# First tile of a fused retention and two-expert-layer kernel: unread products of zeros, k's decays by TensorE, small transfers on ScalarE's queue, v and the next k loaded ahead of the decay matrix

## The chip, the cores and the metric

One program on one core of a Trainium2 chip (8 cores). The metric is the device time of one execution in microseconds (us); the time before is a median of three executions. The profile is one further execution, taken with the hardware profiler.

The engines are TensorE (PE in the rows; PEld is its weight load), VectorE (DVE), ScalarE (ACT), GpSimd (POOL) and SyncE (SP). "SPq" marks an instruction in which SyncE issues a transfer (DMA). Each engine runs its own instructions in the order in which they are written; an instruction waits until its operands are ready, and all behind it on that engine wait too.

## The reference

Inputs: q, k, v of shape (2, 8, 768, 64), one decay `lam` per head, and the weights of two mixture layers of 8 experts. All is float32.

```python
for b in range(nb):                       # blocks of one sequence (block = 64)
    intra = einsum(qb, kb) * Dmask        # Dmask[i, j] = lam ** (i - j) for i >= j, else 0
    intra = einsum(intra, vb)
    inter = einsum(qb * lam ** (pos + 1), kv_state)
    out[block] = intra + inter
    kb_dec   = kb * lam ** (block - 1 - pos)
    kv_state = lam ** block * kv_state + einsum(kb_dec, vb)
x = out as (1536, 512)
...
logits = x @ w_gate + softplus(x @ w_noise) * noise    # first layer: the best two experts of each row
x = sum over the two of weight * relu(x @ w1[e]) @ w2[e]
...
x = gate * relu(x @ u1[e]) @ u2[e]                     # second layer: the best one, with a capacity
```

## The kernel before, in words

The sequence stage treats 12 tiles of 128 rows (6 for each of the two sequences), with blocks of 128 instead of 64, which computes the same. For tile j the steps are, by the names that the rows show:

- loads of k, q and v (`ldk`, `ldq`, `ldv`; one `ldq` serves two tiles), issued by SyncE, with three buffers for k and v;
- `front(j)`: TensorE transposes k (into the PSUM tile `hp`) and, every second tile, q (`hp<-iw,qp`); ScalarE copies the results to `kT` and `qT`, after bringing q in order (`qp`). GpSimd makes `kd`, which is k times the decays of its rows, and `qd`, which is `qT` times powers;
- `scores(j)`: the products `tr<-qT,kT`; VectorE multiplies them by the decay matrix, `at<-tr,dm`;
- `mix(j)`: the products `yp<-at,ldv` (and, but for the first tile of a sequence, `yp<-qd,st`), which ScalarE copies to `xT`; then `yp<-ldv,kd`, which VectorE adds to the state `st`;
- `rows(j)`: the products `yp<-iw,xT`, which turn the rows back and give the first gate's logits; `xr` is stored to HBM as `x`. `iw` holds the identity and the gates' weights.

`load(j)`, `rows(j - 1)`, `front(j + 1)` and the fetch and conversion of experts' weights (`wst`, loaded by SyncE; ScalarE casts it to `wh`, VectorE makes the rest `wl`) lie between `scores(j)` and `mix(j)`. The order on each engine is made by a scheduler when the kernel is built.

The decay matrix `dm` (128 rows x 8 heads x 128, 512 KB) is built once. `lam` is loaded (`lamb`), VectorE makes its powers by doubling in `pw` (a slice of a buffer called `xg`), SyncE writes 8 rows of them to HBM (`powers`, each followed by a row of zeros), and then reads them back with a start that moves by one element from partition to partition, which gives the matrix with its zeros. The column `dm[:, :, 0:1]` is also what `kd` is made with. `tc.issue_after(x)` sets what follows behind x in the order of issue; it is no wait.

After tile 11 the two expert layers follow, some 560 us of products on TensorE.

Of the kernel before, what the change touches and what calls it, by code (L numbers as in the profile page):

```python
# [20 lines left out]
P = 128  # L21
# [15 lines left out]
def kernel(ctx: ExitStack, tc: tile.TileContext, q, k, v, lam, g1, gn, noise,  # L37
# [105 lines left out]
    def load_v(j):  # L143
        rows_of("v", v, j)

    def load(j):
        load_kq(j)
        load_v(j)
# [14 lines left out]
    nc.gpsimd.affine_select(out=ident, in_=ident, compare_op=OP.not_equal, fill=1.0, base=0,  # L163
                            pattern=[[-1, P]], channel_multiplier=1)
    nc.gpsimd.tensor_copy(iw[:, 1:, G:G + P], ident[:, None, :].to_broadcast([P, DC - 1, P]))


    pw = rt.tile([P, 2, ROW], F32, name="xg", bufs=4).rearrange("p a b -> p (a b)")[:, :H * P]
    pw = pw.rearrange("p (h m) -> p h m", h=H)
    nc.sync.dma_start(powers[:, :, P:], zero[0:1, None, :].to_broadcast([1, H, P]))  # L170
    nc.gpsimd.memset(pw[:, :, P - 1:], 1.0)
    nc.vector.tensor_copy(pw[:, :, P - 2:P - 1], lamb[:, :, None])
    m = 1
    while m < P:
# [2 lines left out]
        nc.vector.tensor_mul(pw[:, :, a - n:a], pw[:, :, P - 1 - n:P - 1],  # L177
                             pw[:, :, a:a + 1].to_broadcast([P, H, n]))
        m *= 2
    written = nc.sync.dma_start(powers[:, :, :P], pw[0:1]).ins  # L180
    with tc.issue_after(written):
        load_v(0)
    dm = aw.tile([P, H, P], F32, name="dm", bufs=1)
    written = nc.sync.dma_start(dm, bass.AP(tensor=powers.tensor, offset=powers.offset,
                                            ap=[[1, P], [2 * P, H], [1, P]])).ins
    with tc.issue_after(written):
        load(1)
    pq = aw.tile([P, HP, P], F32, name="pq", bufs=1)
    dec = consts.tile([P, HP, 1], F32, name="dec")
    half = P // 2  # L190
# [298 lines left out]
    def pair(t, hp):  # L489
        return t[:, 2 * hp:2 * hp + 2, :].rearrange("p a d -> p (a d)")  # L490

    def front_q(j):
# [4 lines left out]
        for g in range(2):  # L497
# [8 lines left out]
            for c in range(2):  # L506
                if j % NC or c:
                    nc.gpsimd.tensor_mul(QD[j][:, hs, c, :], QT[j][:, hs, c, :], pq[:, hs])

    def front_k(j):  # L510
        c = j % NC
        ps = bank("hp", [P, HP, P])
        for hp in range(HP):
            nc.tensor.transpose(ps[:, hp, :], pair(qkv["k", j], hp), ident)
        KT[j] = aw.tile([P, HP, P], F32, name="kT")
        nc.scalar.copy(KT[j], ps)
        if c < NC - 1:
            KD[j] = aw.tile([P, H, D], F32, name="kd")
            kept[j] = nc.gpsimd.tensor_mul(KD[j], qkv["k", j], dm[:, :, 0:1].to_broadcast([P, H, D])).ins

    def front(j):
        front_k(j)
        if j % 2 == 0:
            front_q(j)

    def scores(j):
        qt = QT[j - j % 2]
        ps = [bank("tr", [P, HP, P]) for s in range(2)]
        for hp in range(HP):
            for s in range(2):  # L530
                r = slice(s * D, s * D + D)
                nc.tensor.matmul(ps[s][:, hp, :], KT[j][r, hp, :], qt[r, hp, j % 2, :], start=True, stop=True)
        for s in range(2):
            AT[j, s] = aw.tile([P, HP, P], F32, name="at", bufs=3)
            mixed[j] = nc.vector.tensor_mul(AT[j, s], ps[s], dm[:, s::2, ::-1]).ins
# [123 lines left out]

    tA, tB = slice(0, TA), slice(TA, NT)  # L660
    want(("a", 0), w1[0], w2[0])
    front(0)
    for j in range(NT):
        if j + 2 < NT:
            with tc.issue_after(written):
                load(j + 2)
                if j == 0:
                    nc.sync.dma_start(iw[:, :, :E], g1.rearrange("(c p) e -> p c e", p=P))
                    nc.sync.dma_start(iw[:, :, E:G], gn.rearrange("(c p) e -> p c e", p=P))
                    nc.sync.dma_start(iw[:, :, G + P:], g2.rearrange("(c p) e -> p c e", p=P))  # L670
                    nc.sync.dma_start(nz, noise.rearrange("(t p) e -> p t e", p=P))
        if j == 2:
            with tc.issue_after(kept[1]):
                more_constants()
        scores(j)
        if j:
            rows(j - 1)
        if j + 1 < NT:
# [716 lines left out]
```

## Time and profile before

| | |
|---|---|
| median of 3 executions | 649.7 us (649.18 to 652.34) |
| the profiled execution | 655.0 us, of which 653.2 us are the span from its first to its last instruction |
| TensorE busy | 615.0 us, 94% of the span |
| VectorE / ScalarE / GpSimd busy | 376.1 / 278.9 / 173.9 us |
| granted clock of TensorE, mean of the execution | 0.99 |

Times in the rows are us from the first instruction. A row of the timeline has the start, the busy time, the engine, the line of the kernel, the operation and its tiles (result <- operands), how many instructions are merged into it, and in brackets how long the engine stood idle before it and what ended that. A float32 product of full width shows as two records (x16 for 8 products); a transpose as one.

### The profile page before, as it was taken

To read this page: it belongs to the slowest core of one execution; us is meant where nothing else is said; L and a number is where in the kernel's file an instruction comes from. 1 tells how busy PE (TensorE), PEld (TensorE's weight loads), DVE (VectorE), ACT (ScalarE), POOL (GpSimd) and SP (SyncE) were. 2 spreads that over 40 slices of the span, in tenths; PEclk is the share of its full clock that TensorE was granted. 3 is DMA by queue.
4 is the path that set the end of the run, shared out by engine and by line. 5 is a ranking of instruction groups with operands and counts; after the bars stand their busy time and mean duration, and the time that the engine had idled before them with its cause. 6 is when DMAs were issued, how large, how long until landed. Compare 5 with 4: busy or idle time off the path is not lost. (4 is left out here: it accounts for less than half of the span.)

```text
span 653.2 us, 11244 instructions
## 1 busy us (share of the span) xinstructions
PE 615.0 (94%) x4173; PEld 562.8 (86%) x4173; DVE 376.1 (58%) x841; ACT 278.9 (43%) x481; POOL 173.9 (27%) x197
## 2 busy tenths in 40 slices
PE   3999889989999999999999999999989999999992
PEld 3898877978999999989999999888779989988881
DVE  3375858835545454364544545438777558568880
ACT  2466521135434353343533434135036367466760
POOL 3645610245004021040220101023146135024120
PEclk9999999989999999999999999999999999999997
DMA  6799423355736347565553421182397977757710
GB/s 150 169 300 271 135 85 99 113 160 175 240 98 201 120 113 232 154 185 180 161 168 121 148 66 39 20 294 78 96 335 243 299 239 253 249 192 251 247 38 18
DMA packets 106786, 109.96 MB, mean 168 GB/s; under 512 B 36711, under 2 KB 82807, under 8 KB 106720
## 3 DMA queue, kind: packets, MB, share of 16 engines
q1 hardware_dynamic: 97920, 83.58, 43.0%
q0 software_dynamic: 8800, 25.54, 11.7%
q8 instruction: 36, 0.59, 0.4%
q14 instruction: 30, 0.25, 0.1%
HBM read 92.07 MB, written 17.94 MB: 168 GB/s over the span
## 5 line engine op out<-in xcount | busy, mean ns | idle before, releaser
L111 DVE TENSOR_TENSOR wl<-wst,wh 128x1024 fp32r<-128x1024 f32 x107 | 135.8, 1278 | 60.1 <-ACT wh L105 59.0
L105 ACT CAST wh<-wst 128x1024 fp32r<-128x1024 f32 x107 | 111.4, 1047 | 34.4 <-PE yp L720 28.5
L719 PE MATMUL hp<-x,wh 128*128 128x372 f32 (+9 forms) x352 | 116.9, 333 | 0.8 <-ACTq L1206 0.4
L720 PE MATMUL hp<-x,wh 128*128 128x372 f32 (+9 forms) x352 | 117.2, 334 | 0.0
L721 PE MATMUL hp<-x,wl 128*128 128x372 f32 (+9 forms) x352 | 116.3, 331 | 0.0
L793 ACT ACTIVATE h<-hp 128x372 fp32r<-128x372 f32 (+9 forms) x88 | 41.3, 469 | 172.5 <-PE hp L721 161.3
L719 PE MATMUL yp<-h,wh 128*128 128x372 f32 (+8 forms) x320 | 107.4, 337 | 0.0
L720 PE MATMUL yp<-h,wh 128*128 128x372 f32 (+8 forms) x320 | 106.3, 332 | 1.0 <-DVE h L794 1.0
L721 PE MATMUL yp<-h,wl 128*128 128x372 f32 (+8 forms) x320 | 106.9, 334 | 0.0
L794 DVE SCALAR_TENSOR_TENSOR h<-hp,h 128x372 fp32r<-128x372 f32 (+9 forms) x88 | 46.3, 527 | 64.2 <-ACT h L793 63.5
L719 PEld LDWEIGHTS hp<-x,wh 128*128 128x128 f32 x352 | 66.2, 188 | 2.8 <-issue 0.9
L720 PEld LDWEIGHTS hp<-x,wh 128*128 128x128 f32 x352 | 66.3, 188 | 1.3 <-issue 0.2
L721 PEld LDWEIGHTS hp<-x,wl 128*128 128x128 f32 x352 | 66.2, 188 | 1.3 <-issue 0.9
L469 POOL DMA_INDIRECT xg<-x,Rsrc x25 | 25.6, 1025 | 144.5 <-PE tr L709 125.9
L720 PEld LDWEIGHTS yp<-h,wh 128*128 128x128 f32 x320 | 60.3, 188 | 2.0 <-DVE h L794 1.6
L721 PEld LDWEIGHTS yp<-h,wl 128*128 128x128 f32 x320 | 60.2, 188 | 0.5 <-issue 0.2
L719 PEld LDWEIGHTS yp<-h,wh 128*128 128x128 f32 x320 | 60.0, 188 | 0.7 <-issue 0.4
L711 DVE TENSOR_TENSOR x<-tr,x 128x128 fp32r<-128x128 f32 (+11 forms) x72 | 30.0, 442 | 36.1 <-ACT x L710 31.0
L901 POOL DMA_INDIRECT x<-y,Rdst x25 | 26.2, 1048 | 81.5 <-DVE y L875 77.3
L710 ACT CAST x<-tr 128x128 fp32r<-128x128 f32 (+11 forms) x72 | 26.5, 391 | 44.3 <-PE tr L709 39.4
L866 PE MATMUL tr<-iw,yT 128*128 128x136 f32 (+6 forms) x224 | 35.1, 291 | 2.0 <-DVE y L870 2.0
L866 PEld LDWEIGHTS tr<-iw,yT 128*128 128x128 f32 (+6 forms) x224 | 28.3, 175 | 7.0 <-DVE y L870 2.2
(364 smaller groups left out, 1035.2 us busy)
## 6 DMA issues: line engine op xcount, KB each, us to landing
wst<-in_moe_w_dram SPq DMA_DIRECT2D x107, 512.0 KB
more<-in_moe_w_dram SPq DMA_DIRECT2D x21, 512.0 KB
ldk<-in_k_dram SPq DMA_DIRECT2D x12, 256.0 KB
ldq<-in_q_dram SPq DMA_DIRECT2D x6, 512.0 KB
ldv<-in_v_dram SPq DMA_DIRECT2D x12, 256.0 KB
x<-xr SPq DMA_DIRECT2D x12, 256.0 KB
out_dram<-zero SPq DMA_DIRECT2D x12, 256.0 KB
dm<-powers SPq DMA_DIRECT2D x1, 512.0 KB
```

Of the source, the lines that this page charges most:

```text
L105: nc.scalar.copy(hi, st)
L111: nc.vector.tensor_sub(lo, st, hi.bitcast(F32))
L469: i = nc.gpsimd.indirect_dma_start(out=r, out_offset=None, in_=x, in_offset=bass.IndirectOffsetOnAxis(ap=src(s), axis=0))
L710: a = nc.scalar.copy(hi[:, d, :n], ps[:, :n])
L711: v_ = nc.vector.tensor_sub(lo[:, d, :n], ps[:, :n], hi[:, d, :n].bitcast(F32))
L719: nc.tensor.matmul(ps, a[0], b[0], start=start, stop=False)
L720: nc.tensor.matmul(ps, a[0], b[1], start=False, stop=False)
L721: tail["pe"] = nc.tensor.matmul(ps, a[1], b[0], start=False, stop=stop).ins
L793: tail["act"] = nc.scalar.activation(hh, ps, AF.Relu).ins
L794: tail["dve"] = nc.vector.scalar_tensor_tensor(hl, ps, 0.0, hh.bitcast(F32), op0=OP.max, op1=OP.subtract).ins
L866: nc.tensor.matmul(ps[:m, i, :], self.yT[:, 2 * b + i, s * r:s * r + m], iw[:, 2 * b + i, gates2], start=True, stop=True)
L901: i = nc.gpsimd.indirect_dma_start(out=target, out_offset=bass.IndirectOffsetOnAxis(ap=dst, axis=0), in_=y, in_offset=None, bounds_check=t ...
```

## The change

- Nine products of zeros (`busy(9)`) stand first on TensorE, and six (`busy(6)`) behind the scores of tile 0. Their PSUM bank is read by nobody.
- The decays with which `kd` is made come from 8 products of `pw` with one column of the identity (`decays`), copied by VectorE to `dk`; they stand behind the transposes of the first k. `kd` no longer reads `dm`.
- Four transfers go from SyncE's queue to ScalarE's: the two first gates' weights (16 KB each), the zeros and the powers (4 KB each).
- SyncE issues v of tile 0 and k of tile 1 ahead of `dm`, and `dm` in two halves (one for each parity of the heads) instead of one.

```diff
--- before.py
+++ after.py
@@ -163,11 +163,15 @@
     nc.gpsimd.affine_select(out=ident, in_=ident, compare_op=OP.not_equal, fill=1.0, base=0,
                             pattern=[[-1, P]], channel_multiplier=1)
     nc.gpsimd.tensor_copy(iw[:, 1:, G:G + P], ident[:, None, :].to_broadcast([P, DC - 1, P]))
+    nc.scalar.dma_start(iw[:, :, :E], g1.rearrange("(c p) e -> p c e", p=P))
+    nc.scalar.dma_start(iw[:, :, E:G], gn.rearrange("(c p) e -> p c e", p=P))
 
 
     pw = rt.tile([P, 2, ROW], F32, name="xg", bufs=4).rearrange("p a b -> p (a b)")[:, :H * P]
     pw = pw.rearrange("p (h m) -> p h m", h=H)
-    nc.sync.dma_start(powers[:, :, P:], zero[0:1, None, :].to_broadcast([1, H, P]))
+    nc.scalar.dma_start(powers[:, :, P:], zero[0:1, None, :].to_broadcast([1, H, P]))
+    load_v(0)
+    rows_of("k", k, 1)
     nc.gpsimd.memset(pw[:, :, P - 1:], 1.0)
     nc.vector.tensor_copy(pw[:, :, P - 2:P - 1], lamb[:, :, None])
     m = 1
@@ -177,14 +181,14 @@
         nc.vector.tensor_mul(pw[:, :, a - n:a], pw[:, :, P - 1 - n:P - 1],
                              pw[:, :, a:a + 1].to_broadcast([P, H, n]))
         m *= 2
-    written = nc.sync.dma_start(powers[:, :, :P], pw[0:1]).ins
+    nc.scalar.dma_start(powers[:, :, :P], pw[0:1])
+
+    dm = aw.tile([P, H, P], F32, name="dm", bufs=1)
+    for s in range(2):
+        written = nc.sync.dma_start(dm[:, s::2, :], bass.AP(tensor=powers.tensor, offset=powers.offset + s * 2 * P,
+                                                            ap=[[1, P], [4 * P, HP], [1, P]])).ins
     with tc.issue_after(written):
-        load_v(0)
-    dm = aw.tile([P, H, P], F32, name="dm", bufs=1)
-    written = nc.sync.dma_start(dm, bass.AP(tensor=powers.tensor, offset=powers.offset,
-                                            ap=[[1, P], [2 * P, H], [1, P]])).ins
-    with tc.issue_after(written):
-        load(1)
+        load_v(1)
     pq = aw.tile([P, HP, P], F32, name="pq", bufs=1)
     dec = consts.tile([P, HP, 1], F32, name="dec")
     half = P // 2
@@ -507,16 +511,33 @@
                 if j % NC or c:
                     nc.gpsimd.tensor_mul(QD[j][:, hs, c, :], QT[j][:, hs, c, :], pq[:, hs])
 
+    dk = aw.tile([P, H, 1], F32, name="dk", bufs=1)
+
+    def busy(n):
+
+        ps = bank("yp3", [P, P])
+        for _ in range(n):
+            nc.tensor.matmul(ps, zero, zero, start=True, stop=True)
+
+    def decays():
+        ps = bank("yp2", [P, H, 1])
+        for h in range(H):
+            nc.tensor.matmul(ps[:, h, :], pw[:, h, :], ident[:, 0:1], start=True, stop=True)
+        nc.vector.tensor_copy(dk, ps)
+
     def front_k(j):
         c = j % NC
         ps = bank("hp", [P, HP, P])
         for hp in range(HP):
-            nc.tensor.transpose(ps[:, hp, :], pair(qkv["k", j], hp), ident)
+            i = nc.tensor.transpose(ps[:, hp, :], pair(qkv["k", j], hp), ident).ins
+        if j == 0:
+            with tc.issue_after(i):
+                decays()
         KT[j] = aw.tile([P, HP, P], F32, name="kT")
         nc.scalar.copy(KT[j], ps)
         if c < NC - 1:
             KD[j] = aw.tile([P, H, D], F32, name="kd")
-            kept[j] = nc.gpsimd.tensor_mul(KD[j], qkv["k", j], dm[:, :, 0:1].to_broadcast([P, H, D])).ins
+            kept[j] = nc.gpsimd.tensor_mul(KD[j], qkv["k", j], dk.to_broadcast([P, H, D])).ins
 
     def front(j):
         front_k(j)
@@ -529,7 +550,7 @@
         for hp in range(HP):
             for s in range(2):
                 r = slice(s * D, s * D + D)
-                nc.tensor.matmul(ps[s][:, hp, :], KT[j][r, hp, :], qt[r, hp, j % 2, :], start=True, stop=True)
+                tail["score"] = nc.tensor.matmul(ps[s][:, hp, :], KT[j][r, hp, :], qt[r, hp, j % 2, :], start=True, stop=True).ins
         for s in range(2):
             AT[j, s] = aw.tile([P, HP, P], F32, name="at", bufs=3)
             mixed[j] = nc.vector.tensor_mul(AT[j, s], ps[s], dm[:, s::2, ::-1]).ins
@@ -659,20 +680,22 @@
 
     tA, tB = slice(0, TA), slice(TA, NT)
     want(("a", 0), w1[0], w2[0])
+    busy(9)
     front(0)
     for j in range(NT):
         if j + 2 < NT:
             with tc.issue_after(written):
                 load(j + 2)
                 if j == 0:
-                    nc.sync.dma_start(iw[:, :, :E], g1.rearrange("(c p) e -> p c e", p=P))
-                    nc.sync.dma_start(iw[:, :, E:G], gn.rearrange("(c p) e -> p c e", p=P))
                     nc.sync.dma_start(iw[:, :, G + P:], g2.rearrange("(c p) e -> p c e", p=P))
                     nc.sync.dma_start(nz, noise.rearrange("(t p) e -> p t e", p=P))
         if j == 2:
             with tc.issue_after(kept[1]):
                 more_constants()
         scores(j)
+        if j == 0:
+            with tc.issue_after(tail["score"]):
+                busy(6)
         if j:
             rows(j - 1)
         if j + 1 < NT:
```

How the order of instructions moves is shown at three places. In the rows, a line of the kernel, the operation, the tiles, the shape of the result and the count are given.

On TensorE, the start of the program up to the first products of tile 1's rows or scores (`ldk` marks transposes of k, `qp` of q, `xg` the powers). Before:

```order
L514 MATMUL hp<-iw,ldk 128x128 x4
L502 MATMUL hp<-iw,qp 128x128 x8
L532 MATMUL tr<-qT,kT 128x128 x8
L555 MATMUL yp_250<-ldv,kd 128x128 x3
L514 MATMUL hp<-iw,ldk 128x128 x4
L548 MATMUL yp_239<-at,ldv 64x128 x8
L555 MATMUL yp_250<-ldv,kd 128x128
L532 MATMUL tr<-qT,kT 128x128 x8
```

And now:

```order
L520 MATMUL yp_183<-zero 128x128 x9
L532 MATMUL hp<-iw,ldk 128x128 x4
L525 MATMUL yp_198<-iw,xg 128x1 x8
L506 MATMUL hp<-iw,qp 128x128 x8
L553 MATMUL tr<-qT,kT 128x128 x8
L520 MATMUL yp_252<-zero 128x128 x6
L532 MATMUL hp<-iw,ldk 128x128 x4
L569 MATMUL yp_268<-at,ldv 64x128 x8
L576 MATMUL yp_279<-ldv,kd 128x128 x4
L553 MATMUL tr<-qT,kT 128x128 x8
```

The zeros and the decays are new, and the products with `kd`, three of which stood ahead of tile 1's transposes and of `at` times v, now stand behind both.

On SyncE, its first transfers. Before:

```order
L153 DMA lamb<-in_lam_dram 128x8
L131 DMA ldk<-in_k_dram 128x8x64
L140 DMA ldq<-in_q_dram 128x8x128
L170 DMA powers<-zero 8x1x128
L180 DMA powers<-xg 8x1x128
L131 DMA ldv<-in_v_dram 128x8x64
L184 DMA dm<-powers 128x8x128
L131 DMA ldk<-in_k_dram 128x8x64
L131 DMA ldv<-in_v_dram 128x8x64
```

And now (the powers are on ScalarE's queue, ahead of its copy to `qp`):

```order
L153 DMA lamb<-in_lam_dram 128x8
L131 DMA ldk<-in_k_dram 128x8x64
L140 DMA ldq<-in_q_dram 128x8x128
L131 DMA ldv<-in_v_dram 128x8x64
L131 DMA ldk<-in_k_dram 128x8x64
L188 DMA dm<-powers 128x4x128 x2
L131 DMA ldv<-in_v_dram 128x8x64
L131 DMA ldk<-in_k_dram 128x8x64
```

The first v and the second k stand ahead of the matrix now; the second v and the third k stand behind it as the second k and v did.

On VectorE, from tile 1's product with `dm` on. Before:

```order
L535 TENSOR_TENSOR at<-tr,dm 128x512 x2
L575 TENSOR_REDUCE lgs<-yp_278 128x16
L575 TENSOR_REDUCE lt<-yp_283 128x16
L576 TENSOR_TENSOR lgs<-lgs,lt 128x16
L560 TENSOR_TENSOR st_162<-st_162,yp_334 64x4x64 x2
L535 TENSOR_TENSOR at<-tr,dm 128x512 x2
```

And now:

```order
L556 TENSOR_TENSOR at<-tr,dm 128x512 x2
L596 TENSOR_REDUCE lgs<-yp_307 128x16
L596 TENSOR_REDUCE lt<-yp_312 128x16
L597 TENSOR_TENSOR lgs<-lgs,lt 128x16
L581 TENSOR_TENSOR st_165<-st_165,yp_363 64x4x64 x2
L111 TENSOR_TENSOR wl_84<-wst_71,wh_76 128x1024
L556 TENSOR_TENSOR at<-tr,dm 128x512 x2
```

The first conversion of weights (`wl`) has come ahead of tile 2's product with `dm`; it stood behind it. From the first expert job on, the order of instructions is the same on every engine.

## Rows read from the trace of the kernel before

**Rows 1.** The page: busy us of each engine, share of span, instructions.

```profile
PE 615.0 (94%) x4173; PEld 562.8 (86%) x4173; DVE 376.1 (58%) x841; ACT 278.9 (43%) x481; POOL 173.9 (27%) x197
```

**Rows 2.** Stretches: length, busy us (instructions) per engine, PEclk, DMA share, GB/s.

```profile
6.50:8.00 1.50, 0.27 (x1) 0.27 (x2) 1.21 (x6) 1.37 (x2) 0.00 (x0) 1.00 0.01 3
...
10.00:14.00 4.00, 1.71 (x16) 1.41 (x14) 0.11 (x1) 0.32 (x1) 1.08 (x3) 1.00 1.08 255
23.50:27.50 4.00, 4.00 (x30) 3.28 (x30) 0.81 (x3) 2.31 (x5) 2.77 (x4) 1.00 0.02 7
30.00:70.00 40.00, 39.88 (x408) 35.44 (x407) 24.08 (x50) 25.16 (x44) 19.28 (x20) 1.00 1.10 283
```

**Rows 3.** Timeline up to the decay matrix, every engine but TensorE.

```profile
0.93 0.20 POOL L161 MEMSET zero<- 128x128 f32 x1 [0.29 <-POOLq L1378]
...
4.09 2.39 DVE L177 TENSOR_TENSOR xg<-xg 128x8 f32<-128x8 f32 x7
...
6.57 0.61 SPq L180 DMA_DIRECT2D powers<-xg  x1
6.63 1.05 ACT L494 COPY qp<-ldq 128x1024 f32<-128x1024 f32 x1 [4.41 <-DMA ldq<-in_q_dram]
...
8.36 0.38 SPq L184 DMA_DIRECT2D dm<-powers  x1
...
8.88 0.59 ACT L504 COPY qT<-hp 128x512 f32<-128x512 f32 x1 [0.72 <-PE hp L502]
...
13.89 1.29 DVE L535 TENSOR_TENSOR at<-tr,dm 128x512 f32<-128x512 f32 x2 [6.10 <-DMA dm<-powers]
13.92 2.07 POOL L519 TENSOR_TENSOR kd<-ldk,dm 128x512 f32<-128x512 f32 x2 [2.79 <-DMA dm<-powers]
```

**Rows 4.** Timeline of TensorE up to 20 us.

```profile
5.12 1.09 PE L514 MATMUL hp<-iw,ldk 128*128 128x128 f32 x4 [5.12 <-DMA ldk<-in_k_dram]
...
7.73 1.97 PE L502 MATMUL hp<-iw,qp 128*128 128x128 f32 x8 [1.53 <-ACT qp L494]
...
9.63 2.08 PE L532 MATMUL tr<-qT,kT 64*128 64x128 f32 x16
...
15.04 1.65 PE L555 MATMUL yp<-ldv,kd 128*128 128x128 f32 x6 [3.33 <-POOL kd L519]
...
16.48 1.06 PE L514 MATMUL hp<-iw,ldk 128*128 128x128 f32 x4
...
17.47 1.94 PE L548 MATMUL yp<-at,ldv 128*64 128x128 f32 x16
...
19.76 1.16 PE L532 MATMUL tr<-qT,kT 64*128 64x128 f32 x16
```

**Rows 5.** Timeline of TensorE in tiles 1 and 2.

```profile
23.35 1.09 PE L502 MATMUL hp<-iw,qp 128*128 128x128 f32 x8
...
26.75 0.97 PEld L555 LDWEIGHTS yp<-ldv,kd 128*128 128x128 f32 x8
26.75 1.16 PE L555 MATMUL yp<-ldv,kd 128*128 128x128 f32 x8
...
29.01 1.22 PE L572 MATMUL yp<-iw,xT 128*128 128x144 f32 x8 [0.24 <-DVE st L560]
...
30.07 0.60 PE L514 MATMUL hp<-iw,ldk 128*128 128x128 f32 x4
...
30.50 1.06 PE L543 MATMUL yp<-qd,st 128*128 128x128 f32 x8
...
31.49 1.09 PE L548 MATMUL yp<-at,ldv 128*64 128x128 f32 x16
```

**Rows 6.** Timeline, the first weights of an expert: load and conversion.

```profile
27.23 0.43 SPq L90 DMA_DIRECT2D wst<-in_moe_w_dram  x1
...
31.34 1.04 ACT L105 CAST wh<-wst 128x1024 fp32r<-128x1024 f32 x1
...
32.41 1.23 DVE L111 TENSOR_TENSOR wl<-wst,wh 128x1024 fp32r<-128x1024 f32 x1 [1.34 <-ACT wh L105]
```

## The prediction

> **What bounds the kernel now.** I read the page first: TensorE is busy for 615.0 us, 94% of the span [rows 1]. What happens anywhere is therefore worth what it gives back to TensorE. The change touches only the first tile and what hangs on it, so next I read the timeline from the start.
>
> The reader is to see three things there. First, the matrix `dm` is late: its transfer is issued at 8.36, right behind the landing of the powers, and the first product that reads it starts at 13.89, after VectorE had waited 6.10 us for that transfer [rows 3]. `kd` on GpSimd starts at 13.92 for the same reason [rows 3]. Second, TensorE has ended tile 0's scores at 9.63 + 2.08 = 11.71 and then waits 3.33 us for `kd` [rows 4]. Third, what follows runs in a bad order and slowly: three products with `kd` and the transposes of the next k stand in front, so that `at` times v starts at 17.47 although its operands are there at 13.89 + 1.29 = 15.18; and all of this takes twice as long as later. Three products with `kd` take 1.65, four take 1.16 in tile 1; four transposes take 1.06 and later 0.60; `at` times v takes 1.94 and later 1.09 [rows 4, 5]. Tile 1's scores start at 19.76, and from there the products run at the short times [rows 4]. [...]
>
> From tile 1 on TensorE hardly pauses: between 30 and 70 us it is busy for 39.88 of 40 us [rows 2]. A start of tile 1 that is some us earlier is thus kept, as long as the loads keep up. They move 283 GB/s there, with a DMA share of 1.10, which is near full; but between 23.5 and 27.5 the share is 0.02 [rows 2], so there is room to run ahead.
>
> **The change part by part.** I follow the critical engine through the first tile, with the time at which each step ends.
>
> TensorE: the zeros are set at 0.93 + 0.20 = 1.13 [rows 3]. Nine products at the slow price, 1.65 / 3 = 0.55 each [rows 4], end at 1.2 + 4.95 = 6.15. They are free but for one thing: the transposes of k, which started at 5.12 [rows 4], start at 6.15. That is hidden, since their copy stood behind `qp` on ScalarE, which began at 6.63 [rows 3]. No row shows zeros; I take it that they raise the clock as other products do (the rival is below). Four transposes then take 0.60 [rows 5], to 6.75. The powers are done at 4.09 + 2.39 = 6.48 [rows 3]. A decay product has one column, so its price is its weight loads: eight loads take 0.97 in tile 1 [rows 5], 0.12 each, and eight products of two loads take 1.95, to 8.7 (at the slow clock twice that, 3.9).
>
> ScalarE: the three early transfers are issued while it has nothing to do before 6.63. Their 36 KB move beside the first k and q; q then lands later than 6.63, but `qp` can now start at 7.1 at the earliest, and TensorE takes its result at 8.7, so a landing up to 8.7 - 1.05 = 7.65 is covered. The powers' issue takes 0.61 [rows 3] and stands ahead of `qp`: 6.5 to 7.1. `qp` takes 1.05, to 8.15; the copy to `kT` has the size of the one to `qT`, 0.59 [rows 3], to 8.75. TensorE transposes q from 8.7 in two halves of 1.09 / 2 [rows 5], to 9.25 and 9.8; the two copies to `qT` end at 9.85 and 10.45, and the second half of the scores at 10.45 + 1.16 / 2 = 11.0 [rows 4]. That is 0.7 earlier than before. Six more zeros at 1.16 / 4 = 0.29 [rows 5] end at 12.75, the transposes of the second k at 13.35, if that k is there, and it now has four more us to land.
>
> The matrix: before, the issue of the powers at 6.57 was followed by that of `dm` at 8.36, 1.79 us, with nothing else moving (DMA share 0.01 [rows 2]). Now v and k (512 KB) move at that time. The least is 1.79 again; the most is that the small write waits for all of them, 524 KB / 283 GB/s = 1.85 more [rows 2]. I take 0.4, as 8 rows of 512 B have only to get between others: issue at 6.5 + 1.79 + 0.4 = 8.7. From issue to product `dm` took 13.89 - 8.36 = 5.53 [rows 3], with v right in front of it and k and v behind it, at 255 GB/s for all [rows 2]. Now nothing large is in front, but the same amount behind. The least is 1.85 us of data and the 1.79 of a small transfer, 3.64; the most is 5.53; I take the middle, 4.6, so the second half lands at 13.3. The halves help in that VectorE does the first product meanwhile; the second takes 1.29 / 2 = 0.65 [rows 3], to 13.95.
>
> So `at` times v starts at 13.95 instead of 17.47; with its 1.09 and the 1.16 of the products with `kd` [rows 5], tile 1's scores start at 16.2 instead of 19.76. **This is the main term, 3.6 us.** Its bounds: with the matrix at 6.5 + 1.79 + 3.64 = 11.9 TensorE's own chain (13.35) decides, and the gain is 4.2; with it at 6.5 + 3.64 + 5.53 = 15.7 the gain is 1.2.
>
> `kd` from `dk` costs GpSimd the same 2.07 for the two [rows 3], from about 9 on, and leaves the path; the copy to `dk` is one small operation on a VectorE that waits anyway.
>
> The next stretch: from tile 1's scores to `at` times v of tile 2 it was 31.49 - 19.76 = 11.73 us. The products in it, by their rows, are two scores (1.16), two turns with `iw` (1.22), two groups of transposes of k (0.60), two with the state (1.06), one each of q, `at` and `kd` (1.09, 1.09, 1.16): 11.4, and neighbours overlap by 0.07 (16.48 + 1.06 against 17.47) [rows 4, 5]. So 0.3 to 1.0 us were lost there in an order that split the groups; the new order splits less, but puts VectorE's first conversion of weights ahead of tile 2's product. I take 0.4.
>
> The rest: two 16 KB transfers fewer on SyncE let it come earlier to later loads, hidden. The later conversions of weights move by a place or two; each takes 1.23 [rows 6], in either direction, so I take 0 and keep 1.2 on both sides.
>
> **Sum:** 3.6 + 0.4 = 4.0 us less. The profiled execution took 655.0, so one like it would take 651.0; that execution is 5.3 us above the median of the three, 649.7, from which the same 4.0 give **645.7 us** (0.6% less).
>
> **The rivals.** (a) *The matrix is late because its small write shares the DMA engines.* Against it speaks that it is only 4 KB; for it, that 512 KB are put exactly where the share was 0.01 [rows 2]. In full it gives the lower bound above, 1.2 + 0.4 = 1.6 us less: 648.1. [...]
>
> (b) *The gain is given back to the weights.* The first weights' load is issued at 27.23 and their cast starts at 31.34, 4.1 later [rows 6]. Now the issue follows tile 0's store, at some 16.2 + 1.16 + 1.22, 0.6 for two copies of half the size of the one to `qT` [rows 3] and 0.4 for the store's issue, as that of the weights = 19.6; the weights are there at 23.7, cast and rest (1.04 + 1.23) end at 26.0 [rows 6], and the first product behind them at 26.65, while TensorE wants it at 31.49 - 4.0 = 27.5. So 0.85 us of cover is left. For the rival speaks that loads now follow each other without the pause at 23.5 [rows 2]; each us by which the weights are later than that costs one. At 2 us late, with the later loads holding on to it: 647.1.
>
> (c) *The change costs time: zeros do not raise the clock.* Then everything before tile 1 runs at the slow prices: zeros to 6.15, transposes 1.09 to 7.25, decays 3.9 to 11.15, q 1.97 to 13.1, copy to 13.7, second half of the scores 1.04 to 14.75, six zeros 3.3 to 18.05, k 1.06 to 19.1, `at` 1.94 to 21.05, `kd` 2.2 to 23.25 [rows 4]: 3.5 later than before, 653.2. It decides so if the clock is still low when the six zeros run, at about 15. Milder: if tile 0's scores have raised it by 14.75, what follows takes 1.74, 0.60, 1.09 and 1.16, tile 1's scores start at 19.35, and with the 0.4 of the next stretch the gain is 0.8: 648.9. For the rival speaks that the transposes and scores from 7.73 to 11.71 did not raise the clock, since all products from 15.04 on still ran at the low prices, with a pause of 3.33 between [rows 4]. [...]
>
> **How the numbers follow.** 0.5% of 649.7 is 3.25 us, about what a measurement of this kernel can tell from no change. Chances: the forecast 0.60; (a) 0.15; (b) 0.12; (c) in full 0.05, milder 0.08. The forecast's own range: its best end is 4.2 + 1.0 + 1.2 = 6.4 us less, 643.3; its worst has the matrix issued at 8.7 and read 5.53 later, which leaves 2.6 of the main term: 3.0 less, 646.7. (a), (b) and the milder (c) lie between 647.1 and 648.9, give or take what the conversions do; so 643.3 to 649.5. Faster by over 0.5% is nine tenths of the forecast and a little of (b) and (c): 0.57; slower is (c) in full and what I have not thought of: 0.06; the rest, 0.37, lies within.
>
> **What would show it.** Right: `at` of tile 0 starts near 13, TensorE's wait for `kd` is gone, tile 1's scores start near 16.2 and take about 1.16, and tile 2's `at` times v starts near 27.5. (a) shows as `dm` issued behind 9.5 or read behind 15; (b) as a wait of VectorE for `wh`, or of `wh` for its load, ahead of tile 2's product; (c) as transposes of q that take near 2 us. The number is wrong if tile 1 starts early and the first expert job does not.

## The result, and the profile after

The change makes the kernel slower: 653.79 us median against 649.37 (14 runs of each on one chip), 1.0062 times the time before, 95% interval 1.0047 to 1.0077. Beside each other on another chip it was 1.0088 (1.0072 to 1.0105). The prediction said 645.7, and gave "slower" a chance of 0.06; it was wrong.

The profiled execution of after took 651.05 us, that of before 655.0. Neither is typical (655.0 is above all 14 timed executions of before, whose longest is 652.34, and 651.05 is the second shortest of the 14 of after), so their difference has the wrong sign; a pair profiled on one chip follows below.

The busy line of the page of after, which answers to [rows 1]: TensorE is busy 3.8 us longer. The added products alone are 8.6 us (3.97, 1.95 and 2.71 in its timeline below), so the rest is some 5 us shorter.

```profile
PE 618.8 (95%) x4219; PEld 568.1 (87%) x4219; DVE 374.1 (58%) x842; ACT 279.3 (43%) x481; POOL 172.1 (27%) x197
```

The stretches of after (columns as in [rows 2], the first four lines are the same stretches):

```profile
6.50:8.00 1.50, 1.50 (x16) 1.50 (x15) 1.08 (x5) 0.33 (x1) 0.00 (x0) 1.00 1.28 231
10.00:14.00 4.00, 4.00 (x26) 3.45 (x25) 0.38 (x1) 1.09 (x2) 3.89 (x21) 0.50 0.72 179
23.50:27.50 4.00, 3.99 (x44) 3.53 (x39) 0.84 (x2) 1.30 (x2) 3.36 (x4) 1.00 1.15 309
30.00:70.00 40.00, 38.84 (x396) 34.16 (x397) 23.37 (x51) 24.52 (x41) 17.20 (x20) 1.00 0.93 242
...
4.80:8.10 3.30, 2.56 (x23) 2.31 (x22) 2.65 (x10) 0.43 (x1) 0.00 (x0) 1.00 1.24 263
8.20:15.00 6.80, 6.35 (x37) 5.72 (x37) 1.34 (x3) 2.18 (x4) 6.28 (x30) 0.50 0.67 157
```

Three things are to be seen. The loads fill the holes, as meant (DMA share 1.28 where it was 0.01, 1.15 where it was 0.02). The granted clock is 0.50 from 8.20 to 15.00. (Ahead of that the view shows 1.00 from the start, as it did for the slow first tile of the kernel before; that TensorE was fast at 5.90 is to be seen in the durations that follow, 0.63 for k's transposes instead of 1.09 [rows 4].) And between 30 and 70 us TensorE, which had paused for 0.12 us, now pauses for 1.16.

The timeline of TensorE in after's first tile, which answers to [rows 4]:

```profile
1.19 3.97 PE L520 MATMUL yp<-zero 128*128 128x128 f32 x18 [1.19 <-POOL zero L161]
5.90 0.63 PE L532 MATMUL hp<-iw,ldk 128*128 128x128 f32 x4 [0.74 <-DMA ldk<-in_k_dram]
6.38 1.95 PE L525 MATMUL yp<-iw,xg 128*128 128x1 f32 x16
8.77 1.97 PE L506 MATMUL hp<-iw,qp 128*128 128x128 f32 x8 [0.45 <-ACT qp L498]
10.67 2.08 PE L553 MATMUL tr<-qT,kT 64*128 64x128 f32 x16
12.68 2.71 PE L520 MATMUL yp<-zero 128*128 128x128 f32 x12
15.22 0.60 PE L532 MATMUL hp<-iw,ldk 128*128 128x128 f32 x4
15.75 1.09 PE L569 MATMUL yp<-at,ldv 128*64 128x128 f32 x16
16.78 1.16 PE L576 MATMUL yp<-ldv,kd 128*128 128x128 f32 x8
17.86 1.16 PE L553 MATMUL tr<-qT,kT 64*128 64x128 f32 x16
```

The transposes of k take 0.63 and the decays 1.95, as forecast. Those of q, the scores and the six zeros are slow again, 1.97, 2.08 and 2.71, nearly all of it in the stretch at 0.50. Tile 1's scores start at 17.86 instead of 19.76: a gain of 1.9, not 3.6. Executions differ here: in the three profiles of the kernel before they start at 18.4 to 19.8, in the three of after at 17.4 to 17.9.

The other engines there, to be held against [rows 3]:

```profile
6.42 0.61 ACTq L184 DMA_DIRECT2D powers<-xg  x1
...
9.64 0.92 SPq L188 DMA_DIRECT2D dm<-powers  x2
...
13.62 0.69 DVE L556 TENSOR_TENSOR at<-tr,dm 128x512 f32<-128x512 f32 x1 [5.09 <-DMA dm<-powers]
14.52 0.69 DVE L556 TENSOR_TENSOR at<-tr,dm 128x512 f32<-128x512 f32 x1 [0.21 <-DMA dm<-powers]
```

From the issue of the powers to that of the matrix it takes 3.22 us, where it took 1.79; the second half is read at 14.52, and TensorE could take it at 15.21. TensorE's own chain, with the slow zeros and the transposes of the second k, ends at 15.75.

Then tile 2 in after (timeline of SyncE, ScalarE, VectorE and TensorE, in turn), against [rows 5, 6]:

```profile
21.38 0.43 SPq L90 DMA_DIRECT2D wst<-in_moe_w_dram  x1
...
26.78 1.05 ACT L105 CAST wh<-wst 128x1024 fp32r<-128x1024 f32 x1 [2.31 <-DMA wst<-in_moe_w_dram]
...
27.87 1.23 DVE L111 TENSOR_TENSOR wl<-wst,wh 128x1024 fp32r<-128x1024 f32 x1 [1.98 <-ACT wh L105]
29.12 1.29 DVE L556 TENSOR_TENSOR at<-tr,dm 128x512 f32<-128x512 f32 x2
...
29.87 0.43 PE L569 MATMUL yp<-at,ldv 128*64 128x128 f32 x2 [1.28 <-DVE at L556]
```

The weights' load is issued 5.85 us earlier, but the cast of these weights and VectorE's subtraction now stand ahead of tile 2's product: ScalarE waits 2.31 for the load, VectorE 1.98 for the cast, TensorE 1.28 for the product.

**Both kernels on one chip.** The last two profiled runs of this study (e15 and e16 below) show what became of the gain. The start of tile 1's scores and the first `h` (ScalarE's first result of the first expert job), of the kernel before:

```profile
19.48 1.30 PE L532 MATMUL tr<-qT,kT 64*128 64x128 f32 x16
...
97.94 0.41 ACT L793 ACTIVATE h<-hp 128x288 fp32r<-128x288 f32 x1 [0.28 <-PE hp L721]
```

and of the changed kernel:

```profile
17.40 1.16 PE L553 MATMUL tr<-qT,kT 64*128 64x128 f32 x16
...
104.17 0.41 ACT L816 ACTIVATE h<-hp 128x288 fp32r<-128x288 f32 x1 [0.28 <-PE hp L744]
```

TensorE's waits between 14 and 100 us (us in total, times, longest; the row left out is one of 0.4 right ahead of the first `h`, which in the changed kernel lies behind 100 us), of the kernel before:

```profile
PE yp L555 <- POOL kd L519: 2.8, 1, 2.8
PE yp L572 <- DVE st L560: 1.4, 2, 1.1
PE yp L572 <- ACT xT L551: 1.1, 1, 1.1
PE yp L284 <- DVE mbA L612: 0.4, 1, 0.4
...
```

and of the changed kernel:

```profile
PE hp L506 <- ACT kT L537: 3.2, 2, 1.9
PE yp L569 <- DVE at L556: 2.6, 3, 2.2
PE yp L288 <- DVE mbA L633: 2.1, 1, 2.1
PE yp L593 <- ACT xT L572: 1.5, 2, 0.8
```

Three stretches (columns as above), of the kernel before:

```profile
30.70:34.10 3.40, 3.40 (x41) 2.99 (x41) 1.87 (x5) 2.03 (x3) 0.44 (x1) 1.00 1.21 277
...
60.00:80.00 20.00, 18.75 (x190) 16.45 (x189) 13.82 (x31) 11.94 (x22) 13.63 (x15) 1.00 0.70 183
...
85.30:88.70 3.40, 3.39 (x36) 2.80 (x33) 1.99 (x7) 0.59 (x1) 1.15 (x1) 1.00 0.00 0
```

and of the changed kernel:

```profile
30.70:34.10 3.40, 3.24 (x21) 2.83 (x21) 0.55 (x4) 1.59 (x3) 0.00 (x0) 0.50 0.78 234
...
60.00:80.00 20.00, 16.82 (x169) 15.00 (x168) 10.90 (x24) 10.90 (x20) 9.15 (x12) 1.00 0.77 202
...
85.30:88.70 3.40, 3.40 (x17) 3.10 (x16) 3.24 (x16) 1.16 (x3) 0.00 (x0) 0.51 0.02 8
```

Tile 1's scores start 2.1 us earlier (17.4 against 19.5), and the first `h` of the first expert job 6.2 us later (104.17 against 97.94). From 60 to 80 us alone TensorE pauses for 3.2 us instead of 1.25. The waits behind the start of tile 1 are 9.4 us against 2.9. `mbA` is what the ranks' products read (they number the rows that go to the first expert). Behind two of the waits, the one for `at` that ends at 30.3 and the one for `mbA` that ends at 84.9, the granted clock falls to 0.50 and 0.51 for 3.4 us, in which 21 and 17 products are done instead of 41 and 36. That is 1.7 us each, an estimate: half of the 3.4. 6.5 of further waits and 3.4 for the clock, less the 2.1 gained, make 7.8, a little over the 6.2 measured; the order is not the same, so the sum is not exact. The spans differ by 4.7 (653.1 and 657.8), 1.5 less than that: this execution of the kernel before has two such spells of low clock later on, at 473.8 and 589.8, and the changed one only one, at 140.0.

### The profile page after: what moved, and what is told of

Its sections match the earlier page's. It is cut to its first block, busy times and chain, and to the rows that moved or that the text cites. A ratio compares the mean times of both kernels' runs of the same rounds, so it can differ in the third digit from the quotient of the medians.

```text
span 649.5 us, 11332 instructions
## 1 busy us (share of the span) xinstructions
PE 618.8 (95%) x4219; PEld 568.1 (87%) x4219; DVE 374.1 (58%) x842; ACT 279.3 (43%) x481; POOL 172.1 (27%) x197
## 5 line engine op out<-in xcount | busy, mean ns | idle before, releaser
L111 DVE TENSOR_TENSOR wl<-wst,wh 128x1024 fp32r<-128x1024 f32 x107 | 133.8, 1260 | 59.6 <-ACT wh L105 57.3
L483 POOL TENSOR_TENSOR xg<-xg 128x512 f32<-128x512 f32 (+3 forms) x16 | 25.4, 1590 | 34.2 <-DMA xg<-x,Tsrc 26.2
```

The source lines that it names most:

```text
L111: nc.vector.tensor_sub(lo, st, hi.bitcast(F32))
```

## The experiments

The theories. T1: the change moves the weights' casts, and what VectorE subtracts for them, and the ranks' products, ahead of what TensorE wants first, and that order takes the gain back. T2: the zeros bring more spells (stretches at the low clock), wherever they fall. T3: the zeros are worth what they raise the clock for (in e7: the matrix is late through its small write). T4 came out of the first ten profiles: waits of TensorE bring the spells, so that a wait costs itself and more. The last column of the table is the start of the first `h` in the one profiled execution of a run.

| run | kernel | us | before beside it | ratio, 95% | first `h` at |
|---|---|---|---|---|---|
| e1 | before again | 654.57 | 653.84 | 1.0005 (0.9984–1.0026) | 96.70 |
| e5 | after again | 655.15 | 649.45 | 1.0088 (1.0072–1.0105) | 101.90 |
| e2 | after, no zeros | 651.53 | 653.84 | 0.9960 (0.9937–0.9983) | 98.62 |
| e3, e18 | before + zeros | 650.45, 647.77 | 653.84, 649.16 | 0.9948 (0.9930–0.9965), 0.9975 (0.9959–0.9992) | 95.77, 94.25 |
| e6 | before + decays | 648.52 | 649.45 | 0.9984 (0.9970–0.9997) | 95.98 |
| e7 | before + queues, loads | 649.24 | 649.45 | 0.9998 (0.9986–1.0010) | 96.49 |
| e8 | before + zeros + decays | 647.32 | 649.45 | 0.9966 (0.9950–0.9982) | 94.91 |
| e9 | after, casts held | 649.98 | 649.44 | 1.0009 (0.9986–1.0032) | 97.47 |
| e10 | after, ranks held | 652.42 | 649.44 | 1.0064 (1.0041–1.0086) | 99.69 |
| e4, e11 | after, both held | 653.76, 648.49 | 653.84, 649.44 | 0.9988 (0.9962–1.0014), 0.9987 (0.9973–1.0000) | 96.23, 95.58 |
| e12 | e8 + ranks held | 647.01 | 649.44 | 0.9967 (0.9952–0.9981) | 95.33 |
| e13 | e8 + 12 more zeros | 661.54 | 653.12 | 1.0127 (1.0102–1.0152) | 99.24 |
| e14 | e13 + casts held | 660.46 | 653.12 | 1.0118 (1.0095–1.0141) | 99.17 |
| e15, e16 | before, after, one run each | 654.79, 659.38 | 653.12 | | 97.94, 104.17 |
| e17 | after, no zeros, both held | 646.32 | 649.16 | 0.9954 (0.9933–0.9974) | 94.14 |

**e1, the kernel before once more** (no edit).

> The kernel before, unchanged, to have the granted clock and the span of each of its executions, and a second profiled execution of it. All theories expect 649.4 +- 1 us. Theory T2 (the 4.4 us that the change costs in the median are spells at the low clock somewhere in the run, which the profiled executions show by chance only) expects a mean granted clock of 0.990 or more in nearly every execution, where the changed kernel had 0.982 to 0.988 in most. Theory T1 (the new order of the weights' casts and of the ranks' products costs the time ahead of the first expert job) expects clocks that do not explain the difference. Both expect the profiled execution to have less than the 655.0 of the first one, and the gap at 138 to 145 us to be gone.

The same program took 4.5 to 5.2 us more than in the first comparison, on another chip, so 649.4 +- 1 failed for every theory, and the clock was 0.985 to 0.994. A median counts only beside the kernel before on the same chip. T2's "0.990 or more" did not hold, the profiled execution (655.92) is not shorter than the first one, and the waits near 131 to 141 are not gone.

**e2, the changed kernel without its zeros.**

```
-    busy(9)
     front(0)
...
-        if j == 0:
-            with tc.issue_after(tail["score"]):
-                busy(6)
```

> The changed kernel without its fifteen unread products of zeros. T1: nothing is gained by it, 652 to 655 us, since the order of the casts is still early. T2: the zeros bring the low-clock spells, so 649 to 651 us without them and a clock like that of the kernel before. A third theory, that the zeros are worth what they raise the clock for (T3), expects the first tile to be slower, tile 1's scores behind 19 us, and 654 to 656 us.

T3 falls: tile 1's scores start at 18.05, and the run is not slower. The 651.53 us lie between T2's and T1's, and the ratio on this slower chip, 0.9960, is below what any of the three expected. But this edit also moves the order: VectorE's first subtraction stands behind tile 2's `at` again (27.45, behind 26.24), and TensorE has no wait over 0.3 us between 20 and 75 us. So it does not decide between order and zeros. The first cast starts as early as in after (26.11 there against 26.78), and in e7 too (27.03): where `at` is ahead of the subtraction, the early cast costs nothing.

**e3 and e18, only the zeros, in the kernel before.** The two calls that e2 takes out are put in, with `busy` itself.

> The kernel before with only the fifteen unread products of zeros added, at the same two places. T1: 649 to 650 us, as the order of the casts hardly moves. T2: 652 to 655 us, with a granted clock 0.004 or more below that of the kernel before.

> The kernel before with only the fifteen zeros, a second time. If 0.9948 was the zeros: 0.993 to 0.997 again, with tile 1's scores near 17. If it was the chip of that call: 0.998 to 1.001.

T2 falls in this form: the zeros alone make the kernel faster in both, 0.25 to 0.5%. Tile 1's scores start at 17.0 and 17.1, and the casts stand where they stood. This early start does not rest on an early rise of the clock: in e18 the zeros did not bring it (transposes of k 1.06, of q 1.97, scores 2.08; the products are short from 14.5 on), and tile 1 is as early as in e3. In both, the zeros fill most of the wait for `kd`, and `at` times v, now ahead of the products with `kd`, starts at 14.9 and 15.0 instead of 17.47.

**e4 and e11, the changed kernel with casts and ranks held back**, the same kernel on two chips.

```
+        turned[j] = nc.scalar.copy(KT[j], ps).ins
...
+        logged[j] = nc.vector.tensor_add(lgs[:, j, :], lgs[:, j, :], lt).ins
...
-        for _ in range({3: 1, 4: 2, 5: 1, 6: 2, NT - 1: 2}.get(j, 0)):
-            convert()
-            convert_low()
+        if 2 <= j <= 9:
+            with tc.issue_after(logged[j - 1]), tc.issue_after(turned[j + 1]):
+                convert()
+                convert_low()
...
-        if j == TA:
+        if j == TA + 1:
...
-        ps = ranks_of(mbA, sl, tag)
+        with tc.issue_after(tail["rows"]):
+            ps = ranks_of(mbA, sl, tag)
```

> The changed kernel with the casts of the first weights, and what VectorE subtracts for them, held behind the next k's copy and the logits of the tile before, where the kernel before had them, and the ranks' products held behind the rows of tile 9. T1: the 1.9 us that tile 1's scores are early last until the first expert job, whose first h starts near 96.5 instead of 98.65, and the median is 2 us or more below the changed kernel's, 650 to 652. T2: the start of the first expert job moves, the median stays within 1 us of the changed kernel's 653.8 unless the clock changes.

> The changed kernel with both held back, which was 0.9988 on another chip, now beside the two halves. T4: 0.996 to 1.001, as both waits and the spells behind them are gone. T1: the same as with the casts alone. T2: 1.006 to 1.009.

The first `h` is 0.5 to 2.7 us earlier than in the three profiles of the kernel before. e4's 653.76 is above T1's 650 to 652, but its chip is the slower one of e1; beside the kernel before on their chips the two runs are 0.9988 and 0.9987.

**e9, only the casts held** (the edit above without its last two pieces), **and e10, only the ranks held** (those two alone).

> The changed kernel with only the weights' casts and what VectorE subtracts for them held where the kernel before had them; the ranks' products stay early. T4, formed from the ten profiled executions so far: a wait of TensorE of 1.3 us or more is often followed, 0 to 1.5 us later, by a spell at the low clock of 3.4 us or twice that (12 of the 14 spells between 20 and 630 us begin there, 12 of 33 such waits are followed by one, none of 118 waits of 0.3 to 1.25 us), so that a wait costs itself and, at times, 1.7 to 3.4 us more. The changed kernel has two such waits of its own, 1.3 to 1.9 us for tile 2's at near 30 and 2.1 us for the ranks near 82. T4 expects the first of them gone, no spell near 31, the first expert job's first h near 96 to 98 and 1.003 to 1.006 times the kernel before. T1 (the early casts alone): 0.996 to 1.000. T2 (the zeros bring the spells, wherever): 1.006 to 1.009 as in the changed kernel.

> The changed kernel with only the ranks' products held behind the rows of tile 9; the casts stay early. T4: the wait for the ranks (2.1 us) and the spell behind it are gone, the wait near 30 stays, 1.003 to 1.006 times the kernel before. T1: 1.005 to 1.009. T2: 1.006 to 1.009.

The order of the casts decides: held back, they take the changed kernel from 1.006–1.009 to 1.0009 (1.0064 to 1.0009 on one chip, e10 and e9). The ranks alone bring it to 1.0064, which lies between its two own ratios; beside the casts they are worth 0.2%, with intervals that overlap. TensorE's waits between 14 and 100 us, first of e10 and then of e11:

```profile
PE hp L506 <- ACT kT L537: 3.1, 2, 1.7
PE yp L569 <- DVE at L556: 2.7, 3, 2.1
PE yp L593 <- DVE st L581: 1.0, 1, 1.0
...
```

```profile
PE yp L593 <- DVE st L581: 2.6, 2, 1.6
PE yp L593 <- ACT xT L572: 0.7, 1, 0.7
PE yp L593 <- DVE st L583: 0.6, 1, 0.6
...
```

With early casts TensorE waits for `kT` and `at`, whose makers stand behind a cast that waits for its load (2.31 in after); with late ones neither is in the list, and the first `h` comes at 95.58 instead of 99.69. In e9 the wait for the ranks is left (1.75 us, to 77.8), and the clock falls at 79.9. So T1 holds for this kernel, and T2, which expected 1.006 to 1.009 in all three, falls. T4 on top of it fits the places of the spells, but of its ratios only e11's came true: e9 is below its range, e10 and (below) e12 a little above.

**e5, the changed kernel again** (no edit).

> The changed kernel once more, unchanged, beside the kernel before on the same chip as the runs that follow. If the first comparison holds (1.0062), 1.004 to 1.008 times the kernel before. If it came from the low-clock spells of that hour, which took 647.5 to 657.8 us from one and the same program so far, 0.997 to 1.003.

The first comparison holds, 1.0088 being a little above the range expected. This execution too has spells at 31.7 and 82.9 (granted clock 0.50 in both), just behind the waits for `at` and `mbA`; the first profile of after has neither, and was 2.7 us under its median.

**e6, e7, e8: parts of the change alone.** e6 takes the decays (`decays()`, and `dk` in place of `dm[:, :, 0:1]`); e7 is e2 without these two, so queues and loads alone; e8 is e3 with them.

> The kernel before with only k's decays by TensorE (kd no longer waits for the matrix). T1 (order of casts): the first tile is still ended by the matrix, at times v is not later, the order of the casts does not change, so 0.997 to 1.000 times the kernel before. T2 (low-clock spells): the same, no difference in the clock. If the products of the decays raise the clock by themselves, tile 1's scores start before 18 instead of 19.76 and the ratio is 0.995 to 0.997.

> The changed kernel without the zeros and without the decays by TensorE: only the queues and the order of the loads, v and the next k ahead of the matrix, which comes in two halves. T1: the matrix is no earlier than before, but the later loads and the weights run ahead, the casts stand early, so 1.000 to 1.006. T3 (the matrix is late because its small write shares the DMA engines): its issue behind 9.5 as in the changed kernel, tile 0's product behind 17, and 1.000 to 1.004.

> The kernel before with the zeros and the decays, without the queues and the order of the loads. The zeros alone gave 0.9948. T1: the order of the casts stays late as in the kernel before, the gain of the zeros is kept and the wait for kd falls, so 0.991 to 0.995. T2: the clock is what counts, 0.995 +- 0.002 and a clock like that of the zeros alone.

No part alone costs anything, nor do the pairs tried (zeros with decays here, decays with queues and loads in e2). T1's 0.991 to 0.995 for e8 was too good. e7 settles the matrix: the powers are issued at 6.44, `dm` at 9.66, and its first product starts at 13.56. In e8, with the old queue, it is 6.48, 8.28 and 13.87. So from the issue of the small write to that of `dm` it takes 1.4 us more (3.22 against 1.80), as rival (a) has it; the first half is read 0.3 us earlier than the whole matrix in e8 all the same, the second at 14.46. Whether the loads beside it or the new queue make the difference was not shown, as the queue was not tried without the loads.

**e12, e8 with the ranks held.**

> The kernel before with the zeros and the decays (0.9966), and the ranks' products held behind the rows of tile 9, which takes away its wait of 1.5 us for them near 77. T4: the wait and the spells that follow it in some executions are gone, 0.993 to 0.996, below the zeros and decays without that. T1: 0.995 to 0.997. T2: 0.9966 +- 0.001.

No gain. The wait for `mbA` (1.51 us in e8, up to 77.0) became one of 1.82, up to 76.4, for the state on VectorE, and the clock fell at 77.9 behind it: the stall only changed its name.

**e13 and e14, twelve more zeros,** without the queues: e8 with the lines below, and in e14 with the casts held as in e9.

```
         nc.vector.tensor_copy(dk, ps)
+        busy(6)
...
-                busy(6)
+                busy(12)
```

> The kernel before with the decays and with 27 instead of 15 products of zeros (six more behind the decays, six more behind tile 0's scores), without the changed queues and loads. In its order the casts of the weights stand early, as in the changed kernel, though the loads do not. T1 (the order costs): waits of TensorE for at, kT or the casts between 25 and 80 us, the first expert job's first h 2 to 4 us behind that of the next run, and 1.000 to 1.006 times the kernel before, where 15 zeros gave 0.9966. If the queues' transfers cost it and not the order: 0.993 to 0.997.

> The same with the casts held back behind the next k's copy and the logits of the tile before. T1: 0.993 to 0.997, first h near 94 to 95. If the order costs nothing: the same as the run before within 0.002. If the zeros behind the decays keep the clock up through the first tile: no spell at the low clock between 8 and 12 us, the transposes of q in about 1 us, and 1 to 2 us below the 647.3 of 15 zeros.

A miss for T1: both are 1.2 to 1.3% slower, and holding the casts back changes 0.1%. Whether the clock stays up differs between the two. In e14 it falls at 8.4, just as the zeros behind the decays start, and these and most of the transposes of q run slowly:

```profile
8.28 2.81 PE L514 MATMUL yp<-zero 128*128 128x128 f32 x12
10.88 1.49 PE L502 MATMUL hp<-iw,qp 128*128 128x128 f32 x8
```

In e13, whose order of products up to there is the same, it does not fall, and the same products are short:

```profile
8.29 1.58 PE L514 MATMUL yp<-zero 128*128 128x128 f32 x12
9.71 1.04 PE L502 MATMUL hp<-iw,qp 128*128 128x128 f32 x8
```

So a fast first tile did not save e13: tile 1's scores start at 17.32 there and at 18.95 in e14, and both have the first `h` at 99.2. That is 1.2 to 1.3 us later than in e15, and up to the long pause of the `h` near 470 us 6.6 us (e13) and 3.8 us (e14) more are lost. TensorE's waits of e14 from 410 to 450 us:

```profile
PE hp L742 <- PEq L1229: 2.8, 1, 2.8
PE yp L743 <- DVE h L817: 2.1, 1, 2.1
```

The first is TensorE's own sequencer, at the branch behind the first layer; in the other profiles it is not there, and the second is 0.7 to 1.0. With two spells in e13, at 419.6 and 467.4, they make up most of it. Why twelve products at the start bring them was not tried, so these two runs say little on T1.

**e15 and e16, both kernels on one chip** (no edit; rows above).

> The kernel before, unchanged, profiled beside the changed kernel on one chip. First expert job's first h at 96.5 to 98.5 as in its two profiled executions so far, and none or one spell at the low clock between 20 and 630 us.

> The changed kernel, unchanged, beside it. T1 with the spells behind its waits: first h at 98.5 to 102, and one to three spells at the low clock, so 2 to 5 us above the run before this one. If the difference lies behind the first expert job: first h within 0.5 us of that of the kernel before.

The loss stands ahead of the first expert job, more of it than T1 said (98.5 to 102). The kernel before has two spells between 20 and 630 us, where none or one was expected. With one and the same order the first `h` is at 98.65 where no spell follows the waits, and at 101.90 or 104.17 where two do.

**e17, the changed kernel without zeros, casts and ranks held.**

> The changed kernel without the zeros and with casts and ranks held back. If the zeros are worth what they raise the clock for: the transposes of q and the products up to 16 us at the low prices, 0.998 to 1.001 times the kernel before, no better than with the zeros (0.9987). If they bring nothing or cost something: 0.992 to 0.997.

The zeros bring nothing here: without them the ratio is 0.9954, with them it was 0.9987 and 0.9988 on other chips, with intervals that meet. It is faster than the kernel before, but not clearly better than e2 (0.9960), which has neither zeros nor anything held. Its timeline of TensorE:

```profile
9.84 1.95 PE L506 MATMUL hp<-iw,qp 128*128 128x128 f32 x8
11.72 1.69 PE L553 MATMUL tr<-qT,kT 64*128 64x128 f32 x16
...
17.03 1.16 PE L553 MATMUL tr<-qT,kT 64*128 64x128 f32 x16
```

Tile 1's scores start at 17.03, 0.7 and 1.0 earlier than in e4 and e11, which have the zeros; in e2, with the same first tile, they start at 18.05. So the decays and the loads alone gain in the first tile what the zeros alone do (e3, e18: 17.0 and 17.1), or one us less, and the two gains do not add up.

## Why the prediction was wrong

- **The step that failed** is "A start of tile 1 that is some us earlier is thus kept", with its term for the later conversions, "so I take 0 and keep 1.2 on both sides". I had the new order before me, and saw one conversion ahead of tile 2's product, but priced conversions at their own 1.23 us, not at the wait for a load that comes with them (2.31 in after, 3.25 in e16) and is handed on to `kT`, `at` and TensorE. The 2.1 us gained at tile 1 (e16) became 6.2 us lost at the first expert job. With only the casts held back (e9) the loss is gone but for 0.1%.
- **Rival (b)** had the mechanism and named the sign that came, "a wait of VectorE for `wh`, or of `wh` for its load". Its size was wrong: 2 us late, once, for 647.1 (by its own 0.85 us of cover that would be 646.9). It came at `at` and twice at `kT`, and the ranks' products added a wait of 2.1 that no rival had.
- **The clock behind a wait** was in no step. Two waits of 2.1 to 2.2 us were each followed in e16 by 3.4 us at a granted clock of 0.50 and 0.51, by estimate 1.7 us more each.
- **The main term** failed as well: it was 1.9 instead of 3.6, and with the casts and ranks held the whole change is worth 0.1% (e4, e11), not 0.6%. The clock was to stay up from the first zeros on; it fell at 8.2, so that the transposes of q took 1.97, the scores 2.08 and the six zeros 2.71. That is the sign of rival (c), transposes of q near 2 us, though not with its reason in this execution: k's transposes were short behind the zeros (0.63). In e11 and e18 its reason came too: k's transposes took 1.09 and 1.06. That the long times of the first tile are those of a low clock, and that products raise it, was the author's reading: no row of the kernel before shows it, whose view has 1.00 there. What the runs showed is a granted clock of 0.50 from 8.20 to 15.00 in after, where q's transposes and the scores take as long as they did in [rows 4], and k's transposes behind the zeros that are short in some executions and long in others. The fall at 8.2, behind a pause of 0.74, k's transposes and the decays, was not foreseen. e13 and e14 show it absent and present with one order of products, so what decides stays open.
- **The matrix** was issued at 9.64 instead of 8.7 and its second half read at 14.52 instead of 13.3, which is the first sign of rival (a) (issued behind 9.5) but not its second (read behind 15); TensorE's own chain was later still.
- **Right** were the prices of the decays (1.95) and of k's transposes (0.63 for 0.60). With casts and ranks held and without the zeros, the rest of the change gives 0.9954, near the forecast's 0.6% less; but the forecast had much of its gain from the clock that the zeros were to raise, so that nearness is luck.

## What to carry to other kernels

Where an order of instructions is planned from estimated times, an edit that makes the start earlier moves later work too: look in the new order for each instruction that now stands ahead of the one that the critical engine wants, and price it at the wait that it brings along, not at its own length. A wait on the engine that bounds the kernel may cost more than itself: in e16 two of some 2 us were each followed by 3.4 us at a granted clock of 0.50 and 0.51, by estimate 1.7 more. Parts of a change that are neutral or good by themselves, and in the two pairs tried here, can be bad all together, so read the order of the whole, and time it and its parts beside the kernel before on the same chip.

## What the runs showed of the hardware that was not expected

- In the 20 profiled executions there are 30 spells of low granted clock between 20 and 630 us (0.50 and 0.51 in those of e16 and e5 above), 3.4 us long or twice that. 25 begin 0 to 2.1 us behind the end of a TensorE wait of 1.36 to 2.22 us. There are 75 waits of over 1.25 us, so most were followed by none; nor was any of the 226 waits of 0.3 to 1.25 us. The other five spells stand between 453 and 468 us. That the waits cause them is the reading of these counts and of e9 to e11; a wait was not put in by itself.
- Behind nine products of zeros at the start TensorE is fast in some executions of a kernel and not in others. In the 13 profiled executions that have them, k's transposes take 0.60 to 0.70 in eight; in three (e12, e13, e16) they take 1.06 to 1.09, but those of q are short (1.04 to 1.14); in e11 and e18 all is slow up to the scores (2.08). In ten of the other eleven the granted clock is 0.50 again from some point between 7.6 and 10.3 us on, for 3.4 us or twice that; in e13 it stays up. In the seven without zeros the short durations begin between some 13 and 20 us.
- One and the same program (before) has medians of 649.2 to 649.5 us in four comparisons and 653.1 and 653.8 in two others. In the profiles of the latter the stretch from the fifth to the ninth `h` of the first layer (about 115 to 156 us) takes 40.8 to 43.7 us, in the others 38.0 or 38.1, with TensorE waits of 1 to 2 us near 131 to 141 that the others lack. The first profile of before took 43.7 there and that of after 38.1; these 5.6 us are more than the 3.7 by which their spans differ. What differs between these chips stays open.
